# One output tensor, two of its 64 stores split in two: gK of turns 50 and 56 as 68 and 60 rows

## The chip, the cores and the metric

The kernel runs on one core of a Trainium2 chip. The metric is the device time of one execution in microseconds (us). Three executions of the kernel before gave 885.38, 884.0 and 885.0 us, median 885.0. One more execution was taken with the hardware profiler; it took 885.37 us, and the span from its first to its last instruction is 883.6 us.

The engines are TensorE (PE, its weight loads PEld), VectorE (DVE), ScalarE (ACT), GpSimd (POOL) and SyncE (SP). SP only issues and waits. Transfers between HBM and the on-chip memory (128 partitions, called rows here) are carried by 16 DMA engines, which take packets from queues: q1 holds what SP issues, q0 what POOL issues, q8 and q14 the engines' own instructions.

## The reference

A decode step of a transformer layer (one token, batch 2, width 640, 32 heads of 128, a cache of 4096 positions) followed by its whole backward pass. The outputs are the layer's result and the gradients of x, of the K cache, of the V cache and of four weight matrices.

```python
q = (layernorm(x) @ wq)                       # per head: 1 x 128
scores = einsum("bhqd,bhkd->bhqk", q, k_cache) * Dh ** -0.5
p = softmax(scores)
h = x + einsum("bhqk,bhkd->bhqd", p, v_cache) @ wo
out = h + relu(layernorm(h) @ w1) @ w2
grads = vjp(out)(grad_out)                    # gx, gK, gV, gwq, gwo, gw1, gw2
```

With one query, the gradient of a head's K cache is an outer product: gK = gs x q, a column of 4096 score gradients by a row of 128, and gV = p x go in the same way. Each is 4096 x 128 bf16, 1 MB for each of the 64 pairs of batch and head. So 128 MB of gradients are written, and the caches (64 MB each) are read, V for the most part twice.

## The kernel before

**Layout.** A head's 4096 x 128 block lies in one on-chip tile [128, 32, 128]: partition p holds positions 32p to 32p+31, that is 8 KB which are also 8 KB in a row in HBM (`natural`: `cache[b, h].rearrange("(p sc) d -> p sc d", sc=NSC)`). A load or store of such a tile is one DMA of 128 rows of 8192 bytes.

**Pass 1** (`p1_iter`) takes the 64 pairs in order: it loads K and V, forms the scores and the softmax, and keeps what the backward pass needs. For the last six heads of each batch V stays on chip (`KEPT`).

**Pass 2** (`p2_iter`, one call for each of 64 turns j) loads V again as the tile W where it wasn't kept (52 loads), transposes it on TensorE (`pair_transpose`, L440, copied out by ACT at L445), forms dp = V go (`pair_matvec`, L453), and from it the score gradient `gsp` (`score_grad`, L882). VectorE makes gK and gV as two half tiles each (`outer_half`, L868); a few columns of gV are made by ACT (L958). In call j, gK of turn j-1 is made first, and then gV of turn j. `store` (L887 to L890) issues the DMA and gives the tile back to the pool of 1 MB buffers; a buffer is written again only when its store has landed.

**Who issues.** `alone[0]` is false while pass 1 still runs beside pass 2, and then stores go through POOL's queue. Once pass 1 is over, `alone[0]` is true: SP issues the W loads (L461) and the gV and gK stores (L889) in the order of the program, and POOL issues the rest: the weight gradients (`out_dram<-ot`, L1015), and reloads of w2 (`w_t`) and wq (`wqs`). gK of the first 16 turns goes through POOL, that of turns 16 to 63 through SP. In the trace SP issues gK of turn 50 at 755.4 us and gK of turn 56 at 812.6 us; turns 50 and 56 are heads 12 and 18 of batch 1.

**SP's look-ahead.** SP's DMAs use eight completion semaphores in rotation. Before SP issues a DMA it waits until the one eight issues earlier has landed completely. Thus at most eight of its DMAs are under way.

**The background work.** The order of work is written out by hand: `plan` interleaves the calls of the two passes, and generators (`middle_gen`, `fin_gen`, `gx_gen`) are advanced between the steps of `p2_iter` by rates. In the last 100 us they make the gradient of wq (PE, ACT and POOL's stores of `ot`) and of x (DVE L697). Three small results leave as rows of 256 bytes through SP: `orow` at L692 and L694, of 10 rows at 784.1 us, and of 7 and 3 rows at 843.8 and 846.3 us.

Of the kernel before, what the change touches and what calls it, by code (L numbers as in the profile page):

```python
# [15 lines left out]
def kernel(  # L16
# [20 lines left out]
    nc = tc.nc  # L37
# [35 lines left out]
    def pst(shape, dtype, role, name):  # L73

        k = banks[role].pop(0)
        banks[role].append(k)
        return ps.tile(shape, dtype, tag=f"bank{k}", bufs=1, name=name)
# [12 lines left out]
    def take(tag, shape, name):  # L90
        assert free[tag] > 0, (tag, name)
        free[tag] -= 1
        k = homes[tag].pop(0)
        stored.discard(k)
        t = pools[k].tile(shape, BF16, tag=f"big{k}", bufs=1, name=name)
        home_of[id(t)] = (tag, k, t)
        return t
# [9 lines left out]
    def give(t, to=None, out=False):  # L107
        tag, k, _ = home_of.pop(id(t))
        if out:
            stored.add(k)  # L110
        to = to or goes_to(tag)
        owned[tag] -= 1
        owned[to] += 1
        free[to] += 1
        homes[to].append(k)
        given_at[k] = step[0]
# [252 lines left out]
    alone = [False]  # L369
# [62 lines left out]
    def pair_transpose(nat, g, dve=False, busy=0):  # L432


        t_ps = pst([128, GT // 2, 128], FP32, "tps", "t_ps")
        warm(t_ps[:].rearrange("p j k -> p (j k)"), nat, g, busy)
        natf = nat[:].bitcast(FP32)
        for j in range(GT // 2):
            cc = (g * GT) // 2 + j
            nc.tensor.transpose(t_ps[:, j, :], natf[:, 2 * cc:2 * cc + 2, :].rearrange("p c k -> p (c k)"), ident_f[:])  # L440
        t_sb = mats.tile([128, GT // 2, 128], FP32, tag="XT", bufs=4, name="t_sb")
        if dve:
            nc.vector.tensor_copy(out=t_sb[:], in_=t_ps[:])  # L443
        else:
            nc.scalar.copy(out=t_sb[:], in_=t_ps[:])  # L445
        return t_sb

    def pair_matvec(dst, t_sb, g, vecs):
        v = t_sb[:].bitcast(BF16).rearrange("p j (k two) -> p j k two", two=2)
        for j in range(GT // 2):  # L450
            sc = g * GT + 2 * j
            for par in range(2):
                nc.tensor.matmul(dst[:, sc:sc + 2], lhsT=v[:, j, :, par], rhs=vecs[:, par, :],  # L453
                                 start=(par == 0), stop=(par == 1))

    def natural(cache, b, h):
        return cache[b, h].rearrange("(p sc) d -> p sc d", sc=NSC)
# [407 lines left out]
    def outer_half(dst, row, colp, k, short=0):  # L865
        n = HALF - short
        sl = slice(k * HALF, k * HALF + n)
        nc.vector.tensor_tensor(  # L868
            out=pairs_view(dst[:, sl, :]),
            in0=row.rearrange("p (a two) -> p a two", two=2)[:, None, :, :].to_broadcast([128, n, 64, 2]),  # L870
            in1=colp[:, sl, None, :].to_broadcast([128, n, 64, 2]), op=ALU.mult)

    def last_dp(j, c):

        b, h = turns[j]
        pair_matvec(c["dp"], c.pop("T3"), 3, gom[:, h, b, :, :])

    def score_grad(j, c):

        b, h = turns[j]  # L880
        gsp = small.tile([128, NSC, 2], BF16, tag="gsp", bufs=2, name="gsp")
        nc.vector.scalar_tensor_tensor(  # L882
            out=gsp[:], in0=c["dp"][:, :, None].to_broadcast([128, NSC, 2]), scalar=negdot[:, h, b:b + 1],
            in1=P_bf[:, b * H + h, :, None].to_broadcast([128, NSC, 2]), op0=ALU.add, op1=ALU.mult)
        return gsp

    def store(out_ap, t):  # L887

        (nc.sync if alone[0] else nc.gpsimd).dma_start(out=out_ap, in_=t[:])  # L889
        give(t, out=True)  # L890

    def p2_iter(j, busy, act=0, own_gK=False, early=False):

        c = S2[j] if j < NP1 else None
        p = S2.get(j - 1)
        if p is not None:
            bp, hp = turns[j - 1]
            last_dp(j - 1, p)
            gsp = score_grad(j - 1, p)
        if c is not None:  # L900
            b, h = turns[j]
            go = gom[:, h, b, :, :]

            bank = pst([128, 512], FP32, "sps", "dp_ps")
            for k, col in enumerate((goc, qsc)):
                nc.tensor.matmul(bank[:, 128 + k * 128:256 + k * 128],  # L906
                                 lhsT=col[:, h, b:b + 1].to_broadcast([128, 128]), rhs=ident_bf[:],
                                 start=True, stop=True)
            c["dp"] = bank[:, 0:NSC]
            rb = mats.tile([128, 256], BF16, tag="rb", bufs=3, name="rb")  # L910
            nc.scalar.activation(out=rb[:], in_=bank[:, 128:384], func=ACT.Copy, scale=rt[:, b, h:h + 1])  # L911
            pp = small.tile([128, NSC, 2], BF16, tag="pp", bufs=2, name="pp")
            nc.gpsimd.tensor_copy(out=pp[:], in_=P_bf[:, b * H + h, :, None].to_broadcast([128, NSC, 2]))  # L913
            c.update(rb=rb, pp=pp)
            if act:
                pa = small.tile([128, 8], FP32, tag="pa", bufs=2, name="pa")
                nc.gpsimd.tensor_copy(out=pa[:], in_=P_bf[:, b * H + h, NSC - act:NSC])  # L917
            c["T0"] = pair_transpose(c["W"], 0, busy=busy)
        if p is not None:
            gK = take("g", [128, NSC, 128], "gK")  # L920
            outer_half(gK, p["rb"][:, 128:256], gsp, 0)
        yield
        if early:
            gV = take("g", [128, NSC, 128], "gV")
            outer_half(gV, c["rb"][:, 0:128], c["pp"], 0)
        if p is not None:
            outer_half(gK, p["rb"][:, 128:256], gsp, 1)
            store(natural(out_2, bp, hp), gK)
            del S2[j - 1]
        yield  # L930
        if c is None:
            return
        c["T1"] = pair_transpose(c["W"], 1, busy=busy)
        pair_matvec(c["dp"], c.pop("T0"), 0, go)
        if early:
            outer_half(gV, c["rb"][:, 0:128], c["pp"], 1)
            nc.gpsimd.dma_start(out=natural(out_3, b, h), in_=gV[:])
        yield
        c["T2"] = pair_transpose(c["W"], 2, busy=busy)
        pair_matvec(c["dp"], c.pop("T1"), 1, go)  # L940
        yield
        c["T3"] = pair_transpose(c["W"], 3, busy=busy)
        give(c["W"], "g" if j < H and j != 1 and owned["g"] < 3 else None)
        pair_matvec(c["dp"], c.pop("T2"), 2, go)
        if early:
            give(gV, out=True)
            yield
            last_dp(j, c)
            gsp = score_grad(j, c)
        else:  # L950
            gV = take("g", [128, NSC, 128], "gV")
            outer_half(gV, c["rb"][:, 0:128], c["pp"], 0)
            yield
            if own_gK:
                last_dp(j, c)
            outer_half(gV, c["rb"][:, 0:128], c["pp"], 1, act)
            for k in range(act):
                nc.scalar.activation(out=gV[:, NSC - act + k, :], in_=c["rb"][:, 0:128], func=ACT.Copy, scale=pa[:, k:k + 1])  # L958
            store(natural(out_3, b, h), gV)
            if own_gK:  # L960
                gsp = score_grad(j, c)
            yield
        if own_gK:
            gK = take("g", [128, NSC, 128], "gK")
            outer_half(gK, c["rb"][:, 128:256], gsp, 0)
            yield
            outer_half(gK, c["rb"][:, 128:256], gsp, 1)
            store(natural(out_2, b, h), gK)
            del S2[j]
            yield  # L970
# [202 lines left out]
    def bg_until(mark):  # L1173
        slot[0] = 99
        forced[0] = True
        while mark not in done:
            assert bg and bg_one(bg) >= 0.0, mark
        forced[0] = False

    EARLY = 2  # L1180
    M0_ITERS = 7
    P2_AT = H + 2 + M0_ITERS
    RATES = (0.2, 0.8, 0.2, 0.8, 0.45)
# [62 lines left out]
    for n, (i, j) in enumerate(plan):  # L1246
# [18 lines left out]
        if j is not None:  # L1265
            while g2 is not None:
                p2_step()
            if j < NP1:
                bg_until(("go", *turns[j]))
            g2 = p2_iter(j, 0, 8 if i is None and j <= H else 0, i is not None and plan[n + 1][1] is None, j < EARLY)  # L1270
        if i is None and ("w1", 1) in done and fin is None:
# [93 lines left out]
```

## Time and profile before

| what | value |
|---|---|
| median of three runs | 885.0 us (884.0 to 885.38) |
| the profiled execution | 885.37 us, span 883.6 us |
| PE, DVE, ACT, POOL busy | 83%, 77%, 56%, 19% of the span |
| DMA moved | 361.86 MB, mean 410 GB/s |
| q1 (SP), q0 (POOL) | 82.7% and 15.6% of the DMA engines' time |
| gK stores through SP | 48, median 17.3 us from issue to landing |
| last gK store | issued at 865.9 us |

The page of the profile gives the busy share of each engine, the span in 40 slices of 22 us with the mean busy share of the 16 DMA engines and the GB/s that they moved, the queues, the chain of work that ended last, the costliest groups of instructions, and the DMA issues. The trace behind it can be asked for any stretch: the busy time of each engine, the share of the 16 DMA engines that was busy and the rate. A share of 0.06 is one DMA engine of 16. The trace also has a record of each DMA packet (start, duration, bytes, queue) and of each completion event: every DMA engine that takes part in a DMA adds one event to the DMA's semaphore when its share has landed, and the DMA has landed with the last. A packet's record doesn't say which engine carried it.

### The profile page before, as it was taken

What the parts mean: (1) busy time and instruction counts of PE and PEld (TensorE: products, weight loads), DVE (VectorE), ACT (ScalarE), POOL (GpSimd) and SP (SyncE); (2) the same over time, 40 slices, a digit from 0 to 9 for tenths busy, and PEclk for the clock granted to TensorE, in tenths of its full rate; (3) what the DMA queues carried; (4) which work ended last, traced back from release to release, by engine and by line L of the source; (5) the groups of instructions that cost most, each with busy time, mean ns of one, the idle gap of its engine ahead of it and who ended that gap; (6) DMA issues with size and microseconds to landing.
All of it is one profiled execution on the core that took longest, in us unless ns stands there. A gap on an engine that the chain in (4) does not pass through costs nothing.

```text
span 883.6 us, 24847 instructions
## 1 busy us (share of the span) xinstructions
PE 730.4 (83%) x10143; PEld 609.9 (69%) x10143; DVE 680.6 (77%) x1281; ACT 498.7 (56%) x1292; POOL 171.2 (19%) x291
## 2 busy tenths in 40 slices
PE   4999989999998998878868667777878888968780
PEld 4888878888887887767757556566757766654550
DVE  2666878866887897886787898778878679979861
ACT  1444434445776665545555868776656865656570
POOL 1344433443311010000022111111001111111110
PEclk9999999999999999999995657555555855565555
DMA  9999999999979999999999999999999999999995
GB/s 379 424 420 421 417 417 413 422 417 422 372 300 406 415 424 425 423 424 425 415 402 424 422 425 426 425 424 426 422 404 395 424 421 415 424 424 425 424 425 224
DMA packets 56035, 361.86 MB, mean 410 GB/s; under 512 B 5681, under 2 KB 11505, under 8 KB 15217
## 3 DMA queue, kind: packets, MB, share of 16 engines
q1 hardware_dynamic: 46968, 303.29, 82.7%
q0 software_dynamic: 8912, 56.97, 15.6%
q8 instruction: 80, 1.31, 0.5%
q14 instruction: 35, 0.28, 0.1%
q10 hardware_dynamic: 40, 0.01, 0.0%
HBM read 211.11 MB, written 149.13 MB: 408 GB/s over the span
## 4 chain that ended last, share of the span: by engine, by line
DMA 37%; PE 31%; DVE 18%; ACT 7%; issue 5%; ACTq 0%; SPq 0%; DVEq 0%; POOL 0%; POOLq 0%
DMA Vt<-in_A_v_cache_dram 18%; PE t_ps L440 13%; DMA out_dram<-gV 11%; PE m_ps L476 7%; DVE gV L868 4%; DVE gK L868 4%; DMA out_dram<-gK 4%; DMA Wt<-in_A_v_cache_dram 3%; ACT gV L958 3%; PE s_ps L453 2%; DVE pk L486 2%; PE u_ps L514 2%; DVE gxj L697 2%; ACT t_sb L445 2%; PE dp_ps L453 2%
## 5 line engine op out<-in xcount | busy, mean ns | idle before, releaser
L445 ACT COPY t_sb<-t_ps 128x512 f32<-128x512 f32 x479 | 273.1, 588 | 180.8 <-PE t_ps L440 176.6
L453 PEld LDWEIGHTS <-t_sb 128*128 128x128 bf16 x4096 | 178.2, 102 | 62.9 <-ACT t_sb L445 33.5
L440 PE MATMUL t_ps<-ident_f,Wt 128*128 128x128 f32 x832 | 196.0, 386 | 1.2 <-ACT t_sb L445 1.2
L476 PE MATMUL m_ps<-pk,Vt 128*128 128x129 bf16 x2048 | 170.4, 221 | 22.9 <-DMA Vt<-in_A_v_cache_dram 22.1
L486 DVE TENSOR_TENSOR pk<-Kt,ep 128x2048 bf16<-128x2048 bf16 (+1 forms) x128 | 152.8, 1194 | 45.7 <-ACT ep L540 30.5
L868 DVE TENSOR_TENSOR gK<-rb,gsp 128x2048 bf16<-128x2048 bf16 x128 | 153.1, 1224 | 19.8 <-DMA out_dram<-gV 17.8
L476 PEld LDWEIGHTS <-Vt 128*128 128x128 bf16 x2048 | 124.1, 98 | 54.0 <-issue 28.1
L440 PEld LDWEIGHTS t_ps<-ident_f,Wt 128*128 128x128 f32 x832 | 136.4, 200 | 28.9 <-issue 19.9
L868 DVE TENSOR_TENSOR gV<-rb,pp 128x2048 bf16<-128x2048 bf16 (+1 forms) x128 | 143.1, 1142 | 17.1 <-DMA out_dram<-gV 7.4
L440 PE MATMUL t_ps<-ident_f,Kt 128*128 128x128 f32 x1024 | 151.9, 281 | 2.4 <-DMA Kt<-in_A_k_cache_dram 1.7
L453 PE MATMUL dp_ps<-gom,t_sb 128*128 128x2 bf16 x2048 | 95.6, 168 | 22.6 <-ACT t_sb L445 22.1
L440 PEld LDWEIGHTS t_ps<-ident_f,Kt 128*128 128x128 f32 x1024 | 110.8, 142 | 5.0 <-ACT t_sb L445 2.7
L502 POOL COPY pk<-ep 128x16 bf16<-128x16 bf16 x80 | 83.6, 1046 | 155.1 <-ACT ep L540 73.9
L453 PE MATMUL s_ps<-qm,t_sb 128*128 128x2 bf16 x2048 | 87.0, 163 | 1.5 <-DVE t_sb L443 1.5
L1012 ACT CAST ot<-o_ps 128x512 bf16<-128x512 f32 (+3 forms) x152 | 67.7, 492 | 7.6 <-PE o_ps L1006 6.8
L604 ACT CAST MT<-m_ps 128x128 bf16<-128x128 f32 x64 | 17.0, 266 | 93.8 <-PE m_ps L476 93.7
L913 POOL COPY pp<-P_bf 128x64 bf16<-128x64 bf16 x64 | 34.7, 544 | 141.5 <-DVE gV L868 122.4
L911 ACT ACTIVATE rb<-dp_ps,rt 128x256 bf16<-128x256 f32 x64 | 30.3, 473 | 50.4 <-PE dp_ps L906 50.2
L697 DVE CUSTOM_DVE_ANT_0 hbc<-wo_t,hbc 128x640 bf16<-128x640 bf16 x64 | 53.0, 828 | 0.8 <-ACT hbc L663 0.6
L958 ACT ACTIVATE gV<-rb,pa 128x128 bf16<-128x128 bf16 x152 | 46.5, 391 | 5.7 <-POOL pa L917 3.1
L697 DVE CUSTOM_DVE_ANT_0 gxj<-wqs,gqr 128x1024 bf16<-128x1024 bf16 x40 | 49.0, 1225 | 0.2
L440 PE MATMUL t_ps<-ident_f,Vt 128*128 128x128 f32 x192 | 40.5, 352 | 1.5 <-ACT t_sb L445 1.5
(208 smaller groups left out, 709.4 us busy)
## 6 DMA issues: line engine op xcount, KB each, us to landing
Kt<-in_A_k_cache_dram SPq DMA_DIRECT2D x64, 1024.0 KB, 19.6
Vt<-in_A_v_cache_dram SPq DMA_DIRECT2D x64, 1024.0 KB, 15.6
Wt<-in_A_v_cache_dram SPq DMA_DIRECT2D x52, 1024.0 KB, 16.7
out_dram<-gK SPq DMA_DIRECT2D x48, 1024.0 KB, 17.3
out_dram<-gV SPq DMA_DIRECT2D x47, 1024.0 KB, 17.9
out_dram<-gV POOLq DMA_DIRECT2D x17, 1024.0 KB, 9.8
out_dram<-gK POOLq DMA_DIRECT2D x16, 1024.0 KB, 10.5
wq_t<-in_A_wq_dram SPq DMA_DIRECT2D x5, 1024.0 KB, 7.9
```

What stands on the lines that cost most here:

```text
L440: nc.tensor.transpose(t_ps[:, j, :], natf[:, 2 * cc:2 * cc + 2, :].rearrange("p c k -> p (c k)"), ident_f[:])
L445: nc.scalar.copy(out=t_sb[:], in_=t_ps[:])
L453: nc.tensor.matmul(dst[:, sc:sc + 2], lhsT=v[:, j, :, par], rhs=vecs[:, par, :], start=(par == 0), stop=(par == 1))
L476: nc.tensor.matmul(r["m"][:, 0:129], lhsT=r["V"][:, sc, :], rhs=r["pk"][sc // HALF][:, sc % HALF, 0:129], start=(sc == 0), stop=(sc == NSC ...
L486: nc.vector.tensor_tensor(out=p["pk"][k][:, 0:n, 0:128].rearrange("p s (a two) -> p s a two", two=2), in0=p["K"][:, sl, :].rearrange("p s ...
L502: nc.gpsimd.tensor_copy(out=col, in_=e)
L697: nc.vector.tensor_tensor_reduce(out=junk[0:kc, 0:width], in0=in0, in1=in1, scale=1.0, scalar=0.0, op0=ALU.mult, op1=ALU.add, accum_out=acc)
L868: nc.vector.tensor_tensor(out=pairs_view(dst[:, sl, :]), in0=row.rearrange("p (a two) -> p a two", two=2)[:, None, :, :].to_broadcast([128 ...
L911: nc.scalar.activation(out=rb[:], in_=bank[:, 128:384], func=ACT.Copy, scale=rt[:, b, h:h + 1])
L913: nc.gpsimd.tensor_copy(out=pp[:], in_=P_bf[:, b * H + h, :, None].to_broadcast([128, NSC, 2]))
L958: nc.scalar.activation(out=gV[:, NSC - act + k, :], in_=c["rb"][:, 0:128], func=ACT.Copy, scale=pa[:, k:k + 1])
L1012: nc.scalar.copy(out=ot[0:P, k, n0:n0 + nn], in_=o_ps[0:P, 0:nn])
```

## The change

`store` gets a row number `cut`. With it, the tile goes out as two DMAs from the same queue, first rows 0 to cut-1 and then rows cut to 127; without it, one DMA of 128 rows as before. `p2_iter` passes 68 when the gK is that of turn 50 or turn 56. Both are issued by SP. No byte more or less is written, and nothing else differs.

```diff
-    def store(out_ap, t):
-        (nc.sync if alone[0] else nc.gpsimd).dma_start(out=out_ap, in_=t[:])
+    def store(out_ap, t, cut=0):
+        eng = nc.sync if alone[0] else nc.gpsimd
+        if cut:
+            eng.dma_start(out=out_ap[0:cut], in_=t[0:cut])
+        eng.dma_start(out=out_ap[cut:128], in_=t[cut:128])
         give(t, out=True)
...
-            store(natural(out_2, bp, hp), gK)
+            store(natural(out_2, bp, hp), gK, CUT if j - 1 in CUT_AT else 0)
...
     EARLY = 2
+    CUT = 68
+    CUT_AT = (50, 56)
```

## Prediction

> **What bounds the kernel now.** I read the page's slices first, then its last issues, then the windows of the tail, and last what SP waits for.
>
> ```profile
> DMA  9999999999979999999999999999999999999995
> GB/s 379 424 420 421 417 417 413 422 417 422 372 300 406 415 424 425 423 424 425 415 402 424 422 425 426 425 424 426 422 404 395 424 421 415 424 424 425 424 425 224
> ```
>
> The DMA engines are full from slice to slice at about 425 GB/s, and only the last slice (861.5 to 883.6 us) is half empty. So the question is what happens in that slice. The windows give PE, PEld, DVE, ACT and POOL busy, then PEclk, DMA share, GB/s:
>
> ```profile
> 784.00:812.00 28.00, 18.21 (x141) 12.10 (x141) 27.64 (x38) 13.80 (x28) 4.10 (x4) 0.58 1.01 426
> ...
> 864.00:868.00 4.00, 0.00 (x0) 0.00 (x0) 0.52 (x1) 0.00 (x0) 0.00 (x0) 0.50 1.02 425
> 870.00:872.00 2.00, 0.00 (x0) 0.00 (x0) 0.00 (x0) 0.00 (x0) 0.00 (x0) 0.50 0.80 336
> 872.00:874.00 2.00, 0.00 (x0) 0.00 (x0) 0.00 (x0) 0.00 (x0) 0.00 (x0) 0.50 0.38 162
> 874.00:876.00 2.00, 0.00 (x0) 0.00 (x0) 0.00 (x0) 0.00 (x0) 0.00 (x0) 0.50 0.20 86
> 876.00:878.00 2.00, 0.00 (x0) 0.00 (x0) 0.00 (x0) 0.00 (x0) 0.00 (x0) 0.50 0.07 29
> 878.00:880.00 2.00, 0.00 (x0) 0.00 (x0) 0.00 (x0) 0.00 (x0) 0.00 (x0) 0.50 0.06 25
> 880.00:882.40 2.40, 0.00 (x0) 0.00 (x0) 0.00 (x0) 0.00 (x0) 0.00 (x0) 0.50 0.06 24
> ```
>
> From 865 us on nothing computes. At 872 six engines of 16 still work (0.38), and from 877 to the end one alone (0.06 is 1/16). The completion events of the last store say it exactly: the first engine is done at 870.95 us, the 15th at 876.57, the 16th at 882.57. Put as lags behind the first they are 0, 0.1, 0.2, 0.5, 0.6, 1.46, 1.47, 1.52, 1.54, 1.8, 3.95, 4.0, 4.1, 4.3, 5.6 and **11.62 us**. I call the last engine S. It has worked without a gap since 755 us; per 1 MB store it spends 2.57 to 2.62 us where the others spend 2.45 to 2.47 (8 packets of 8192 B, one each 306 ns). So the kernel ends when S has worked off its share, 6.0 us after the next engine.
>
> ```profile
> SPq L889 <- DMA out_dram<-gK: 19.4, 7, 3.5
> SPq L889 <- DMA out_dram<-gV: 18.5, 7, 3.6
> ...
> 859.14 0.33 SPq L889 DMA_DIRECT2D out_dram<-gK  x1
> 862.06 0.33 SPq L889 DMA_DIRECT2D out_dram<-gV  x1
> 865.93 0.33 SPq L889 DMA_DIRECT2D out_dram<-gK  x1
> ```
>
> SP (waits of 790 to 884 us, and its last issues) mostly waits for older stores to land: the issue at 865.93 follows S's landing at 865.87 of the store issued eight earlier. DVE's last gK ends at 864.5 and S reaches it only about 878, so compute has some 13 us in hand.
>
> **What the change moves.** No byte goes away. What changes is which engine carries which row. Short stores in this trace tell how: a DMA of 128 or 64 rows gives 16 completion events, `orow` of 10, 7 and 3 rows gives 10, 7 and 3, each with equal shares. So the number of engines is a divisor of the rows, and the largest up to 16 fits all of these. For 68 rows it is 4 engines of 17 rows (17 is too many), for 60 rows 15 engines of 4 rows.
>
> The Trainium skill, page "DMA: Bandwidth & Descriptors", section "Why a DMA increments its semaphore by 16 and not by 1", states this rule, and adds that SP's transfers use the lowest-numbered engines; by that the piece of 68 rows always burdens the same four. The events of 10, 7 and 3 rows agree; no run here shows the numbers of the engines.
>
> Per cut head, instead of 8 rows each:
> - the four carry 17 + 4 = 21 rows, 13 more: 13 x 0.306 = +3.98 us;
> - eleven others carry 4: -1.22 us; S among these saves 4 x 0.325 (its 2.60 us by 8) = -1.30 us;
> - one engine carries none: -2.45 us.
>
> Two heads: the four +7.96 us, S -2.60 us if it isn't one of the four.
>
> Which are the four? When each short `orow` store landed, set beside the lags of the 16 engines at that moment, tells which lags belong to its set. The sets are nested. The 3 rows are on three engines with end lags 0, 0.1 and 1.5, and not on S: that store's last event came at 852.54. The 7 rows (last event 866.20, S's time) add two engines with lag about 1.5, one with about 4.0 (call it X), and S. The four are the three plus one of those four. This is read from time matches and is the weakest step. Two of the four candidates have lag 1.5: then the four end at most at 1.54 + 7.96 = 9.5, and S at 11.62 - 2.60 = 9.02. The last engine is one of the four, 9.5 instead of 11.62: **gain 2.1 us**. So both end nearly together, which is also where more cutting would lose.
>
> Other terms. Each cut adds one SP issue of 0.33 us; it lies in SP's waits (38 us in the last 94 for stores alone), at nothing. It also takes one more of the eight semaphores. The fast engines run 11.6 us = 4.7 stores ahead of S, so of eight DMAs under way they still have 3.3 before them; with a DMA that gives twelve engines nothing, 2.3, at nothing; without that cover, an engine would idle up to 2.45 us, but only one far ahead of S. The buffer is given back when both pieces have landed; the 68 rows land late on the four by 4 to 8 us, while S lets every whole store land later still. DVE, ACT, PE and POOL get no instruction more.
>
> The cost not shown as such is **two engines reading the same rows' memory**: with 17 rows in place of 8, an engine goes to rows that another engine reads for the next whole store. The nearest row on one side is a 64-row load (`w_t`, 80 KB, carried at 137 to 139 us), on the other the only 64-row store (`ot`, 80 KB, 618.5 to 619.6 us):
>
> ```profile
> 132.00:134.00 2.00, 2.00 (x34) 1.99 (x32) 1.98 (x4) 0.86 (x4) 0.00 (x0) 1.00 1.02 430
> 137.00:138.00 1.00, 1.00 (x25) 1.00 (x23) 1.00 (x1) 0.04 (x1) 1.00 (x1) 1.00 0.97 376
> 138.00:139.00 1.00, 1.00 (x15) 0.99 (x13) 0.96 (x5) 0.60 (x3) 0.32 (x2) 1.00 1.07 366
> ...
> 617.00:618.00 1.00, 0.50 (x8) 0.53 (x8) 0.34 (x3) 0.00 (x0) 0.24 (x1) 0.50 1.01 423
> 618.00:619.00 1.00, 1.00 (x15) 1.00 (x14) 0.28 (x1) 0.88 (x3) 0.00 (x0) 0.50 1.01 414
> 619.00:620.00 1.00, 1.00 (x8) 0.94 (x7) 0.56 (x1) 0.80 (x3) 0.00 (x0) 0.50 1.00 417
> ```
>
> With the load the rate falls from 430 to 376 and 366 while the share stays at 1: packets took 353 to 492 ns, 3.0 to 3.7 us of engine time lost for 3.07 us of data, so a row there costs about double. With the store it falls from 423 to 414 and 417, 15 KB in two us: 0.2 per byte or less, and the packets stay at 309 ns. A gain from it is excluded, as no packet can be faster than 306 ns. I take the store's row, at nothing, as the pieces are stores; at 0.2 per byte the four would lose 0.2 x 21 x 0.306 = 1.3 us per head, 2.6 us, all of the gain and half a us more. The load's price is the rival below.
>
> Sum against the profiled execution: 885.37 - 2.1 = 883.3 us (its span 883.6 to 881.5, and 1.8 us around it). That execution is 0.4 above the median 885.0, so against the median 882.9. Own range: 882.3 (the added engine has a lag of less than 1.5) to 885.5 (collisions at 0.2).
>
> **The rivals.**
> 1. *The fourth engine is X*: 4.0 + 7.96 = 12.0 instead of 11.62, +0.4: 885.4. For it: X is in the set of 7. Against: one of four candidates.
> 2. *The fourth engine is S itself*: each head costs it 13 x 0.325 = 4.2, together +8.4: 893.4. For it: S is in the sets of 7 and 10; against: one of four. Neither can be excluded, as the matches don't order the four within the set.
> 3. *The other side: collisions cost as in the load.* Place: the four, while they read 21 rows of a cut head that others read too. Doubled, they lose (42 - 8) x 0.306 = 10.4 us per head, 1.5 + 20.8 = 22.3 at the end, +10.7 us. Spread evenly over all 16 engines instead, 2.45 us per head: the four 9.5 + 4.9 = 14.4, +2.8 us. The load's slowed packets were on many engines, not on four, which lies between: I take the middle, +6.7: 891.7. It decides from (11.62 - 9.5)/2 = 1.1 us per head on, that is 0.17 per row.
> 4. *The pieces are spread evenly over 16 engines*, so that the change doesn't do what its row numbers say: no engine's load moves, 885.0. Against: 10, 7 and 3 events.
>
> The same page of the Trainium skill, section "Rules for kernel authors", advises one 128-partition transfer and not two to disjoint parts, since the two share the engines and serialize; by it nothing would be gained, which is the time of rival 4. The trace agrees that a 64-row transfer uses all 16, but 10, 7 and 3 rows don't.
>
> **How the numbers follow.** Forecast 0.42; X 0.14; S 0.16; collisions 0.20; even 0.08. What this measurement can tell from no change is 0.2%, 1.8 us: under 883.2 is faster. The forecast lies 0.3 below that, and small collisions would take it over; I count 0.32 of the 0.42 as faster, 0.10 as the same. Same: 0.10 + 0.14 + 0.08 = 0.32. Slower: 0.16 + 0.20 = 0.36. The range runs from 882.2 to 893.5: it holds the forecast, X, even, S, and most of the collisions' 887.8 to 895.7; some 0.1 is left out.
>
> **What would show it.** The 68-row DMAs would have 4 events for landed shares, the 60-row ones 15. If S is relieved, the last store's 16th event comes 2.1 us sooner, with four or five events within 2 us of it in place of one, and the share in the last 6 us at 0.25 or more, not 0.06. If S is one of the four, a share of 0.06 stretches over some 14 us. Collisions would show as packets well over 309 ns right after 755.4 and 812.7 us, and as a fall of the rate under 415 there. I am wrong if the fourth engine is another one, or if S's slowness moves with the rows and not with the engine.

## The result and the profile after

| | before | after |
|---|---|---|
| median (six executions each, one chip) | 884.36 us (883.9 to 885.38) | 890.83 us (889.05 to 893.71) |
| ratio | | 1.0072, interval 1.0058 to 1.0086 |
| profiled execution, span | 885.37 us, 883.6 us | 889.98 us, 888.2 us |
| last store, first and last completion event | 870.95 and 882.57 us | 876.29 and 887.28 us |

The change makes the kernel 0.7% slower; a gain of 2.1 us was forecast. The page's last rows of section 2, DMA share and GB/s by slices of 22 us, after:

```profile
DMA  9999999999989999999999999999999999999995
GB/s 378 425 419 420 419 417 410 423 417 421 367 300 416 425 424 424 423 426 424 411 412 424 422 427 424 425 425 425 423 405 396 425 421 415 402 394 423 403 395 221
```

Up to the last slice the share reads 9, as before but for one slice early on. From the 35th slice (755 us, where turn 50 is cut) the rate falls all the same, in four of five slices, to 402, 394, 403 and 395 GB/s. Engines that are busy and yet move less: that is not seen in the row of shares, only in the row below it. The windows around the two cuts show it finer (busy PE, PEld, DVE, ACT, POOL; PEclk, DMA share, GB/s), first before, then after:

```profile
768.00:780.00 12.00, 10.56 (x92) 8.25 (x90) 10.63 (x16) 7.99 (x22) 1.79 (x3) 0.50 1.02 427
780.00:794.00 14.00, 7.32 (x89) 6.37 (x87) 9.74 (x14) 6.13 (x14) 1.10 (x1) 0.69 1.01 421
...
832.00:844.00 12.00, 11.13 (x90) 7.80 (x89) 7.02 (x10) 7.76 (x16) 0.24 (x1) 0.50 1.01 425
```

```profile
768.00:780.00 12.00, 10.77 (x99) 8.55 (x99) 10.23 (x16) 7.75 (x22) 1.65 (x3) 0.50 1.00 378
780.00:794.00 14.00, 8.36 (x92) 7.33 (x90) 11.85 (x16) 7.09 (x15) 1.10 (x1) 0.57 1.00 379
794.00:820.00 26.00, 21.79 (x150) 13.54 (x150) 25.86 (x36) 16.40 (x32) 5.05 (x5) 0.53 1.01 425
...
832.00:844.00 12.00, 10.21 (x91) 6.76 (x89) 3.30 (x5) 9.06 (x19) 0.36 (x2) 0.64 0.95 384
```

The rate is down to 378 and 379 GB/s while and after the pieces of turn 50 are carried (their events lie between 769 and 785 us), is whole again at 425 from 794 to 820, and is down to 384 with those of turn 56 (825 to 844 us). In the packet records an 8192-B packet normally takes 309 ns; between 770 and 780 us 40 of 330 such packets take over 450 ns, 16 of them 596 to 680 (twice as long) and 6 over 1000; before it is 3 of 399. I call a packet slow when it takes over 1.1 times what is usual for its size. Summed over all slow packets of 2 KB and more after 745 us, the time beyond the usual is **57 us of engine time after, 7 us before**; the difference is 3.1 us on each of 16 engines.

The second loss is idle engines. Two windows, first before, then after:

```profile
838.00:850.00 12.00, 11.52 (x87) 7.62 (x85) 9.36 (x12) 9.32 (x19) 2.00 (x3) 0.50 1.01 424
850.00:860.00 10.00, 8.86 (x62) 5.55 (x62) 6.24 (x7) 6.64 (x14) 0.71 (x1) 0.50 1.01 423
```

```profile
838.00:850.00 12.00, 11.52 (x86) 7.55 (x86) 3.07 (x4) 8.46 (x18) 0.77 (x2) 0.50 0.96 389
850.00:860.00 10.00, 7.45 (x57) 4.77 (x54) 7.64 (x9) 6.59 (x13) 1.12 (x3) 0.50 0.89 367
```

The share falls from 1.01 to 0.96 and 0.89: the engines that are ahead have used up what SP was allowed to issue, because the eighth-older DMA hasn't landed on the slowest one (the gK store at 842.50 us is issued right after the 68-row piece has landed at 842.44). They are not the engines that end last, so this is a sign of how far the slowest lags and not itself the loss. The tail, after:

```profile
874.00:876.00 2.00, 0.00 (x0) 0.00 (x0) 0.00 (x0) 0.00 (x0) 0.00 (x0) 0.50 0.99 418
876.00:878.00 2.00, 0.00 (x0) 0.00 (x0) 0.00 (x0) 0.00 (x0) 0.00 (x0) 0.50 0.33 139
878.00:880.00 2.00, 0.00 (x0) 0.00 (x0) 0.00 (x0) 0.00 (x0) 0.00 (x0) 0.50 0.32 135
880.00:882.00 2.00, 0.00 (x0) 0.00 (x0) 0.00 (x0) 0.00 (x0) 0.00 (x0) 0.50 0.22 94
882.00:884.00 2.00, 0.00 (x0) 0.00 (x0) 0.00 (x0) 0.00 (x0) 0.00 (x0) 0.50 0.10 41
884.00:886.00 2.00, 0.00 (x0) 0.00 (x0) 0.00 (x0) 0.00 (x0) 0.00 (x0) 0.50 0.06 25
```

Five engines of 16 (0.33, 0.32) instead of one work on after the others are done. The last store's last five events are at 880.42, 881.74, 882.42, 883.46 and 887.28 us. The last engine is no longer S, the one that ended last before. The events at turn 56 show which it is: the 68-row piece (four events besides one at the issue) lands at 836.90, 837.54, 838.09 and 842.44 us. S had landed the store ahead of it at 835.21 and lands its 4 rows of the 60-row piece at 836.52, 1.31 us later, so it has no share of the 68 rows. One of the four, T, lands its 60-row share at 844.10, 7.6 us behind S, and stays last to the end. T landed the store ahead at 833.59 us at the latest (the last but one of its events), so its 17 rows took at least 842.44 - 833.59 = 8.9 us, where 17 x 0.306 = 5.2 us was counted. POOL's queue moved nothing from 832 to 844 us, so its packets are not the reason.

### The profile page after: what moved, and what is told of

The parts are those of the page before. It is cut to its first block, busy times and chain, and to the rows that moved or that the text cites. A ratio compares the mean times of both kernels' runs of the same rounds, so it can differ in the third digit from the quotient of the medians.

```text
span 888.2 us, 24849 instructions
## 1 busy us (share of the span) xinstructions
PE 733.0 (83%) x10143; PEld 612.7 (69%) x10143; DVE 680.7 (77%) x1281; ACT 498.5 (56%) x1292; POOL 170.8 (19%) x291
## 3 DMA queue, kind: packets, MB, share of 16 engines
q0 software_dynamic: 8912, 56.97, 15.6%
q8 instruction: 80, 1.31, 0.5%
## 4 chain that ended last, share of the span: by engine, by line
DMA 48%; PE 27%; DVE 14%; ACT 5%; issue 3%; SPq 1%; DVEq 0%; POOL 0%; ACTq 0%; POOLq 0%
DMA Vt<-in_A_v_cache_dram 18%; DMA out_dram<-gK 13%; PE t_ps L440 11%; DMA out_dram<-gV 11%; PE m_ps L476 7%; DMA Wt<-in_A_v_cache_dram 5%; DVE gV L868 4%; DVE gK L868 4%; ACT gV L961 3%; PE s_ps L453 2%; DVE pk L486 2%; PE u_ps L514 2%; DMA Kt<-in_A_k_cache_dram 2%; DVE hbc L697 1%; ACT t_sb L445 1%
```

## The experiments

The theory from the traces, A: in a piece, rows are read by other engines than in a whole store, and engines whose rows meet in this way slow each other; this costs every engine some 3 us, and the four more. Rivals: B, only the row counts matter; C, the look-ahead of eight is the loss; D, two DMAs for one, or engines out of step, are slow in themselves.

**Pieces with no shift of rows.**

```diff
-    CUT = 68
+    CUT = 64
```

> Both heads are cut into 64 and 64 rows, so that each piece goes to 16 engines of 4 rows and no engine has more rows than before. Theory A, collisions of the pieces' reads with whole stores: the pieces still read rows that other engines own, with a loss of 10 to 30 us of engine time per head, that is 0.6 to 2 us on every engine: 885.5 to 888.5 us. Theory B, rows alone: as before, 884.4 within 0.5, no packets over 330 ns beyond the few of before. Theory C, look-ahead: each head takes two of eight places instead of one, all of full width: 884.4 to 885.

Measured: ratio 1.0042 (1.0030 to 1.0054), +3.7 us; the median, 889.16, lies 0.7 us above A's range. B falls: no engine has a row more than before, and the kernel is slower all the same. The same rate windows:

```profile
768.00:780.00 12.00, 11.02 (x99) 8.98 (x96) 7.34 (x12) 7.70 (x21) 0.91 (x2) 0.52 1.01 397
...
820.00:832.00 12.00, 7.07 (x65) 5.05 (x63) 11.93 (x20) 5.75 (x13) 3.63 (x4) 0.50 1.01 371
832.00:844.00 12.00, 9.55 (x96) 7.58 (x94) 7.70 (x15) 7.82 (x16) 0.49 (x2) 0.64 1.01 408
```

Full shares at 397, 371 and 408 GB/s; 52 us of engine time in slow packets. The slow packets aren't only the pieces': the 7680-B packets of an uncut weight-gradient store, carried in 760 to 790 us beside the first two pieces, take up to 1133 ns, where before they took 291 ns as a rule and 327 at most.

**Two DMAs, but by columns.** Each piece has all 128 rows with half of their bytes.

```diff
-            eng.dma_start(out=out_ap[0:cut], in_=t[0:cut])
-        eng.dma_start(out=out_ap[cut:128], in_=t[cut:128])
+            eng.dma_start(out=out_ap[:, 0:cut], in_=t[:, 0:cut])
+        eng.dma_start(out=out_ap[:, cut:], in_=t[:, cut:])
...
-    CUT = 68
+    CUT = 16
```

> The gK of turns 50 and 56 go out as two DMAs again, but cut by columns: each piece has all 128 rows with half of their bytes, 4096 B. So there are two DMAs and two places of the look-ahead as in the changed kernel, but each row is read by the engine that reads it in a whole store. Theory A, collisions (rows read by an engine other than the one that has them in whole stores): no packet slowed, time as before within 0.5 us. Rival D (two DMAs in place of one, smaller pieces or the engines' getting out of step slow the transfers): a loss as with the halves by rows, 2 to 5 us.

Measured: 1.0001 (0.9989 to 1.0013); 6 us of slow packets, as before the change. The same windows:

```profile
768.00:780.00 12.00, 10.57 (x89) 7.42 (x88) 11.93 (x19) 7.09 (x18) 2.73 (x5) 0.50 1.01 426
...
820.00:832.00 12.00, 6.86 (x67) 5.92 (x66) 11.10 (x21) 5.21 (x12) 1.89 (x3) 0.50 1.02 422
832.00:844.00 12.00, 10.86 (x87) 6.92 (x85) 6.77 (x9) 8.39 (x18) 0.26 (x2) 0.50 1.01 425
```

D falls: a second DMA, a second place of the look-ahead and packets of half the size cost nothing that can be measured. What is left as the cost is which engine reads which row; the traces show it by the slow packets, not by the engines' numbers, which a packet's record doesn't have.

**On the chip or in HBM?** The pieces are the two halves of the HBM block, as with 64 and 64 rows, but each is read from all 128 rows on the chip.

```diff
-            eng.dma_start(out=out_ap[0:cut], in_=t[0:cut])
-        eng.dma_start(out=out_ap[cut:128], in_=t[cut:128])
+            for hf in (0, 1):
+                eng.dma_start(
+                    out=out_2[cut][hf * 2048:(hf + 1) * 2048].rearrange("(p sc) d -> p sc d", sc=16),
+                    in_=t[:, hf * 16:(hf + 1) * 16])
+        else:
+            eng.dma_start(out=out_ap, in_=t[:])
...
-            store(natural(out_2, bp, hp), gK, CUT if j - 1 in CUT_AT else 0)
+            store(natural(out_2, bp, hp), gK, (bp, hp) if j - 1 in CUT_AT else 0)
```

> Turns 50 and 56 again in two DMAs each. In HBM the pieces are the same two halves as with 64 and 64 rows (512 KB in a row each), but on the chip each piece is read from all 128 rows, 4096 B of each, so that every engine reads its usual rows. The order of the values within gK of these two heads is therefore not the right one; work and bytes are the same. Theory A1, the collisions are on the chip (two engines at the same rows): no packet slowed, 884.7 within 0.6 us, as with the cut by columns. Theory A2, the collisions are in HBM (which engine writes which part of a head's 1 MB): a loss as with the halves by rows, 3 to 5 us.

Measured: 0.9990 (0.9981 to 0.9998), not slower; 13 us of slow packets. The same windows:

```profile
768.00:780.00 12.00, 10.87 (x100) 8.64 (x100) 10.12 (x16) 7.75 (x22) 1.62 (x2) 0.50 1.02 416
780.00:794.00 14.00, 7.99 (x89) 6.98 (x87) 12.04 (x16) 6.95 (x15) 1.14 (x2) 0.70 1.01 418
...
832.00:844.00 12.00, 10.86 (x87) 6.92 (x84) 6.72 (x9) 8.39 (x17) 0.31 (x2) 0.50 1.01 425
```

So the collisions are on the chip, A1: the same halves in HBM cost 3.7 us when they are read from 64 rows each, and nothing that shows in the time when they are read from 128. Around turn 50 the rate is a little lower than before (416 and 418 against 427 and 421 GB/s); what those few slow packets come from is open.

**More of them.** Sixteen heads in halves:

```diff
-    CUT = 68
-    CUT_AT = (50, 56)
+    CUT = 64
+    CUT_AT = tuple(range(40, 56))
```

> The gK of sixteen turns, 40 to 55, are cut into 64 and 64 rows. Theory A, collisions: every cut head pays its own price; the two heads of turns 50 and 56 cost 4.2 us together, 2.1 per head, so 16 heads cost up to 34 us, 919 us; by the 10 us of engine time that the first of those two lost (0.6 us on each engine) 16 heads cost 10 us, 895. Rival D (the loss comes from engines being out of step, which doesn't grow with the number of cuts): under 892.

Measured: 1.0232 (1.0216 to 1.0248), +20.5 us or 1.3 us per head, between the two prices named; 211 us of slow packets after 745 us. The first of these heads is cut at 669 us; counted from 650 us on it is 339 us, against 45 before, which makes 18.4 us on each engine, most of the 20.5. One window of it:

```profile
794.00:820.00 26.00, 14.91 (x123) 10.70 (x123) 23.28 (x32) 11.20 (x23) 3.15 (x4) 0.57 0.98 355
```

So each cut head pays. Of the 39 us of engine time that 1 MB takes unhindered (2.45 x 16), 1.3 x 16 = 21 us come on top, 0.5 of the pieces' own time ("per byte", as the prediction has it); in the two halves it is 3.7 x 16 / 78 = 0.8. Counted by slow packets alone it is (339 - 45) / (16 x 39.2) = 0.5 and (52 - 7) / 78 = 0.6.

**One cut alone**, 68 and 60 rows, at turn 50 and at turn 56.

```diff
-    CUT_AT = (50, 56)
+    CUT_AT = (50,)
```

> Only the gK of turn 50 is cut (68 and 60 rows). Theory A, collisions: while the 68-row piece is carried, packets take about twice their 309 ns, for the four engines and for those whose rows they read; at turn 50 the changed kernel lost some 18 us of engine time in that way between 770 and 780 us, so all engines come about 1.1 us later and the four by 4.0 + 2 to 3: the last engine is S at 11.6 - 1.3 + 1.1, no change, or one of the four at 10 to 11: 883 to 886 us, against 884.4 before. Theory B, rows alone: no packet is slower and only the 8-against-21 rows count: S saves 1.3 us and stays last, 883.1. Theory C, look-ahead: the loss is idle engines that wait for the eighth-older DMA; it needs both cuts, because with one the slowest engine is never later than S was: 883 to 884.4, and no idle stretch between 840 and 860.

```diff
-    CUT_AT = (50, 56)
+    CUT_AT = (56,)
```

> Only the gK of turn 56 is cut. Theory A, collisions: about 10 us of engine time lost between 831 and 843 us, and one of the four, T, ends at a lag of 4 + 4.0 + 4.4 = 12.4 instead of S at 11.6: 884.5 to 886 us. Theory B, rows alone: S saves 1.3: 883.1. Theory C, look-ahead: as with turn 50 alone, 883 to 884.4; if the idle engines between 840 and 860 us are still there, they come from turn 56 alone and not from the sum of two cuts.

Measured: 0.9999 (0.9989 to 1.0008) and 0.9999 (0.9990 to 1.0008): no change, and so within A's times; B's 883.1 is missed. The slow packets after 745 us are 36 and 15 us, against 7 before. In the trace with turn 56 alone S lands its 4 rows 1.30 us after the store ahead (836.63 and 837.93 us) and is last at 881.80, 0.8 us sooner than before: relief less collisions. A's account of this run is missed all the same: it put T last, at a lag of 12.4 us, but the engine next to S ends at 877.50 us, 4.3 us ahead of S. (That execution took 884.54 us, close to its median of 884.77; the profiled one with turn 50 alone took 888.64 us, 3.4 above its median, and isn't read for its end.) Nothing and nothing make 6.5 us when both are cut: a single cut uses up only part of the room that the four have ahead of S, and with the second T ends behind S, as the trace of the change shows. Theory C would fit the single cuts as well, but not the halves: there the loss stands in windows with a full share (371 GB/s at 1.01), in which no engine waits for SP.

**At the very end**, where less is being carried beside it. Only the last gK is cut:

```diff
-    CUT_AT = (50, 56)
+    CUT_AT = (63,)
```

> Only the very last gK (turn 63) is cut into 68 and 60 rows. When it is carried most engines have nothing behind it, so little can collide and nothing waits for its landing. S saves 4 rows, 1.3 us; the four end 4.0 us later, at lags of 1.5 to 8.2. All theories: S stays last at 10.3, 883.1 us; theory A allows up to 1 us of collisions on top for the four, which doesn't show. If T had a lag over 6.5 before, it would end last and the time would not fall.

Measured: **0.9976 (0.9966 to 0.9986)**, 2.1 us faster than the kernel before. Its tail:

```profile
876.00:878.00 2.00, 0.00 (x0) 0.00 (x0) 0.00 (x0) 0.00 (x0) 0.00 (x0) 0.50 0.13 53
878.00:880.00 2.00, 0.00 (x0) 0.00 (x0) 0.00 (x0) 0.00 (x0) 0.00 (x0) 0.50 0.06 20
880.00:882.00 2.00, 0.00 (x0) 0.00 (x0) 0.00 (x0) 0.00 (x0) 0.00 (x0) 0.50 0.01 4
```

S is still alone from 878 on, but ends at 880.71 us. It landed the gV ahead at 879.48 and its 4 rows 1.23 us later. The 68-row piece had landed at 876.55, before S was even at it: S is none of the four. Slow packets come to 14 us after 745 us, against 7 before, so even there the cut isn't free of collisions.

The control, the last gK in halves:

```diff
-    CUT = 68
-    CUT_AT = (50, 56)
+    CUT = 64
+    CUT_AT = (63,)
```

> Only the very last gK is cut, into 64 and 64 rows, beside the cut at 68 there, which gained 1.5 to 2.1 us. No engine gets more or fewer rows: S has 8 as before. Theory: the gain at 68 was S's 4 rows less; here there is none: 884.7 within 0.6, up to 1 us more by collisions. Rival: two shorter DMAs at the end are themselves better (the last landing or the completion is sooner): 883.2.

Measured: 1.0012 (1.0001 to 1.0023). No gain: what gains at 68 is S's four rows, not the shorter DMAs. Other cuts there, 116 and 12 rows, and 102 and 26:

> The very last gK alone is cut, into 116 and 12 rows: four engines of 29 rows and twelve of one row. By rows alone S has 1 row where it has 4 with the cut at 68: 1.0 us sooner, 882.3; the four carry 30 rows in place of 21 and end 2.8 us later than with the cut at 68, where they ended 2.9 to 5.5 us ahead of S: they come level with S, 882.3 to 883. With collisions among the four, which read the same parts while all others are done, up to 2 us more: 885.

Measured: 0.9982 (0.9973 to 0.9990), faster than before too, and within the interval of the cut at 68. S lands its one row at 879.96 us and the four theirs up to 879.73: level, so there is no more to gain in this way.

> The very last gK alone is cut, into 102 and 26 rows: by the divisors 6 engines of 17 rows and 13 of 2 rows. It asks whether S is among the first six. If it is, it carries 19 rows instead of 8: 3.6 us later than before the change, 888. If it isn't, it carries 2 rows, 2.0 us sooner than with a whole store, and the six with 3.4 us more than before still end ahead of it: 882.5. S is none of the four (it landed later than the 68-row piece) and is in the set of seven, so two places of three are inside: 888 is the likelier.

Measured: 1.0050 (1.0038 to 1.0062), +4.4 us, median 888.6. S is one of the first six: its share of 17 rows lands at 883.44, 5.37 us after the gV ahead (878.07), alone for the last 7 us. So S is among the first six and not among the first four: the fifth or the sixth, if DMAs of few rows take the engines in one fixed order, as the nested sets of the prediction have it.

And two cuts at the end:

```diff
-    CUT_AT = (50, 56)
+    CUT_AT = (62, 63)
```

> The gK of the last two turns, 62 and 63, are cut into 68 and 60 rows. By rows S saves 2.6 us in place of 1.3: S would end 2.6 us sooner than without a cut, 882.1. The four carry 8 us more; with one cut at the end they were done 2.9 to 5.5 us ahead of S (877.8 against 880.7), so another 4.0 us without relief for S would bring them to 881.8, beside S at 879.4: one of the four ends last, 2 to 3 us later by collisions, since the gK of turn 62 is carried while others still store: 884 to 887. If collisions cost nothing there: 883 to 884.

Measured: 1.0010 (0.9996 to 1.0023), no gain left. The profiled execution took 889.34 us, 4 above the median, so it shows the order and not the typical size: S lands its last rows at 880.11 us, sooner than in any trace above but the one with 116 rows, and the four at 879.58, 882.70, 883.93 and 886.64. Its tail:

```profile
880.00:882.00 2.00, 0.00 (x0) 0.00 (x0) 0.00 (x0) 0.00 (x0) 0.00 (x0) 0.50 0.19 78
882.00:884.00 2.00, 0.00 (x0) 0.00 (x0) 0.00 (x0) 0.00 (x0) 0.00 (x0) 0.50 0.13 49
884.00:886.00 2.00, 0.00 (x0) 0.00 (x0) 0.00 (x0) 0.00 (x0) 0.00 (x0) 0.50 0.05 20
```

Three engines, then two, then one, after S is done. S is relieved as counted, and engines of the four take its place. Slow packets are 27 us after 745 us, with the two heads cut at the end.

## Why the prediction was wrong, point by point

- *What bounds the kernel: one engine, S, at the end.* Right: taking 4 rows from S at the very end gains 2.1 us, giving it 11 more loses 4.4.
- *How many engines carry how many rows.* Right: 68 rows gave 4 events for landed shares, 60 gave 15, 116 and 12 gave 4 and 12, 102 and 26 gave 6 and 13. The Trainium skill, page "DMA: Bandwidth & Descriptors", section "Why a DMA increments its semaphore by 16 and not by 1", has this rule (the largest divisor up to 16); these events agree with it.
- *S saves 1.30 us per cut and is not one of the four.* Right: 1.23 to 1.31 us for its 4 rows in four traces, and with the cut at the very end the 68-row piece had landed before S was at it.
- *"I take the store's row, at nothing, as the pieces are stores."* **This step failed.** The term of two engines reading the same rows was set at nothing, with 0.2 per byte as its upper end; it measured 0.5 (sixteen heads) to 0.8 (two heads), and T's 17 rows at turn 56, 8.9 us in place of 5.2, lie between with 0.7. The row taken was one 80-KB store; the row next to it, the load at about 1 per byte, was nearer. Why that 64-row store went by without slow packets stays open; it wasn't tried with one of that size through POOL. By the measured price the four lose 0.5 to 0.8 x 21 x 0.306 = 3.2 to 5.1 us per head: 1.5 + 7.96 + 6.4 to 10.2 = 15.9 to 19.7 at the end in place of 11.62, +4.3 to +8.1 us; measured are +6.5.
- *The forecast's own condition, that the fourth engine has a lag of 1.5.* Left open: T's share of the 68 rows can't be told apart, as to where it began, from a small lag with collisions.
- *The look-ahead at nothing.* Wrong in part: the share fell to 0.89 for 10 us. It didn't set the end, as T was last.
- *The rivals.* What came about is the third, with the place (the four) and the sign that it named; its middle, 891.7, lies 0.9 us above the measured 890.83. That closeness is in part luck: it is the mean of two ways to spread the loss, and the price that it took, about 1 per byte, was above the measured one. Its chance of 0.20 was too small for a price whose two nearest rows lay so far apart: the forecast stood or fell with the lower one, and it left only (11.62 - 9.5)/2 = 1.1 us per head for it.
- *Readings of the tail.* Three are off, and the forecast doesn't turn on them. S reaches the last gK at 880.14 us, when the store ahead has landed on it, not at 878, so compute had 15.6 us in hand. At 872 us eleven engines still work; 0.38 is the mean from there to 874. And S's 2.57 to 2.62 us per store hold while the others are busy: its last four stores follow each other by 2.43 to 2.46 us, as on other engines.

The Trainium skill bears on the mechanism. Its page "SBUF — State Buffer", section "Door 1: The DMA port swizzle", says that a partition's number decides through which of 16 ports a DMA reaches it, and the Trainium skill's page "DMA: Bandwidth & Descriptors", section "The descriptor swizzle", says that in a transfer of 128 partitions each engine has one port for itself. The two cuts that keep 128 rows (1.0001 and 0.9990) and the halves of 64 rows (1.0042) agree with that; the ports themselves no run here shows. By the Trainium skill's page "DMA: Bandwidth & Descriptors", section "Rules for kernel authors", two transfers to disjoint partition halves gain nothing, since they serialize. The runs agree that nothing is gained, but the measurement goes further: they cost, 1.0042 for two heads.

## What to carry to other kernels

When all DMA engines are busy, read the GB/s beside the share: here a full share at a lower rate was engines slowing each other, and pieces whose rows were read by other engines than usual paid for it with half their time or more again. If a transfer in flight beside others has to be cut, try a cut by columns (1.0001 here) before one by rows (1.0042); a cut by rows to shift work between engines paid only at the very end, and there for one store only. And where one term decides the sign and its two nearest rows are far apart, the forecast is the middle, not the row that suits the change.

## What was not expected of the hardware

- Two DMAs of 128 rows and half of the bytes were as fast as one (1.0001), while two of 64 rows cost 0.5 to 0.8 of their own time.
- One of the 16 engines ends 11.6 us behind the first and 6.0 us behind the next in the kernel before, and the same place in the order (fifth or sixth) fits all traces that tell. Beside busy engines it needs 2.57 to 2.62 us for a store where the others need 2.45 to 2.47, but at the end, when the others are done, 2.43 to 2.46; where it lost its time wasn't tried.
- Single cuts and double cuts differ by more than their sum (0 and 0 against 6.5 us), which fits an end that is the maximum over engines.
